# Gated linear attention with a maxout FFN: other score products, paired head parities, and FFN steps given out in thirds

## The chip, the core and the metric

The kernel runs on one core of a Trainium2 chip. The core has five engines that run side by side, each through its own list of instructions in order: TensorE (matmuls; PE in the profile, and PEld for its weight loads), VectorE (DVE), ScalarE (ACT), GpSimd (POOL) and SyncE (SP), whose queue issues all transfers here. They meet only at semaphores: an instruction that waits holds back everything behind it on its own engine. Matmuls write to PSUM, which this kernel cuts into four buffers of two banks; the other engines empty them. The metric is the device time of the program in microseconds (us).

## What is computed

```python
# q, k, v, a_re, a_im: (batch 4, heads 8, seq 768, head_dim 48); w1..w3: (384, 768); w_out: (768, 384)
mag = sqrt(a_re**2 + a_im**2)
scale = minimum(mag, 0.999) / (mag + 1e-6)
ar, ai = a_re * scale, a_im * scale              # a complex gate per step and key channel
for t in range(768):
    S_re, S_im = ar*S_re - ai*S_im + outer(k[t], v[t]), ar*S_im + ai*S_re
    y[t] = q[t] @ S_re
x = y as (4*768 tokens, 8*48)
out = maximum(maximum(x @ w1, x @ w2), x @ w3) @ w_out
```

## The kernel before

The recurrence is worked in chunks of 64 steps. A tile `x` is 128 tokens (two chunks) of one batch element, all 8 heads; a group `g` is two tiles of the same place in two batch elements (x = 2g and y = 2g + 1). There are 24 tiles and 12 groups, and 6 groups follow each other along one sequence.

For each tile there is this work, by the functions of the code:

- `gate_steps`, `turns`, `sines`, `products`: from the gates come log magnitudes `Ln`, running angles (matmuls `cs`), sines `CS`, magnitudes (matmuls `sums`, exponentials `En` and `E`), and with them the keys and queries `Uk` and `Uq`, 112 columns per head. `products(x)[2]` multiplies `Uk` by `En` once the keys have been turned.
- `turn`: PE transposes `Uk` and `Uq` (tiles `tp`), and ACT copies them out to `K` and `Q`.
- `cut`: 16 small matmuls `F` and four exponentials on ACT give `f`, the decay factors between positions within a chunk. Its columns are found by the constants C8 to CD; NF of them in all.
- `prep`, parts 0 to 3 on DVE: `Q`, `K` times factors. They write 16 more columns into `Q` (two products), the keys `KB`, the queries `QB` (two products) and `QG`.
- `scores`: PE makes `A` (from `K` and `Q`, 32 matmuls with 48 columns) and `B` (from `KB` and `QB`, 32 with 80 columns), each into 32 partitions.
- `gather`: DVE moves the blocks that count into the score tile `atm` with masked copies, two from `A` and three from `B`.
- `state`: matmuls `dk` and DVE operations `g` (times the factors, plus `dk`) carry the state on.
- `outputs`: matmuls `y`, 64 per tile, from `atm` with the values `vb` and from `QG` with the state `g`. A pass over 32 output channels that straddles two heads needs two of each kind. ACT copies the result to `xT`.
- The FFN of the group before: `up_step` (three weights by two halves of the 768 channels, 9 matmuls of 128x256 each, then ACT's copy or DVE's maximum into `hT`) and `out_step` (6 matmuls `op`, ACT's copy to `ot`, one transfer out).

A matmul in f32 shows in the profile as two records, so 32 matmuls are x64 there.

The order is written out by hand from group 2 on for PE (`T["chain"]`); on the other engines, and in the groups 0 and 1, a scheduler decides. `group(g)` puts FFN steps between the parts of the attention with `feed(n)`, which takes n steps from a list of eight: one at the start of the group, one after `pairs(x)`, one after the sums, two inside `turning` (ahead of `cs`), two after `pairs(y)`, and one after `turned(y + 1)`. `pairs(x)` is `scores` A, B and `gather` A, B. `turned(x)` is turn keys, turn queries, `cut`, `state` of the tile before, and `prep` part 0. So PE's list in a steady group reads: `op`, A, B, `up`, tp, tp, F, dk, sums, sums, `up`, y, `up`, `up`, cs, A, B, `up`, `up`, tp, tp, F, dk, `op`, y. The exponentials and logarithms of the group after next (`later`, two of three gate steps) stand on ACT between the sines and the copy of the second pair of turned tiles.

A PSUM buffer is handed from use to use. The build fixes which instruction each first matmul waits for: before the change the `up` behind the sums waits for ACT's exponentials `f`, and the `op` behind the second dk waits for ACT's copy `K`.

Of the kernel before, what the change touches and what calls it, by code (L numbers as in the profile page):

```python
# [51 lines left out]
def kernel(  # L52
# [15 lines left out]
    P = 128  # L68
# [15 lines left out]
    C8, C8B, C16, C32, CK, CG, CD, NF = 0, 4, 8, 12, 20, 28, 36, 37  # L84
# [83 lines left out]
    masko = const.tile([P, 4, 32], U8, name="masko")  # L168
# [4 lines left out]
    vbs = [const.tile([P, 2, H // 2, P], FP, name="vb%d" % i) for i in range(4)]  # L173
# [3 lines left out]
    us = {nm: [const.tile([P, H, 2, L64], FP, name="u%s%d" % (nm, i)) for i in range(n)] for nm, n in (("k", 3), ("q", 2))}  # L177
    fs = [const.tile([P, H, 2, NF], FP, name="f%d" % i) for i in range(2)]
    KB = const.tile([P, H, P], FP, name="KB")

    def constants_early():
# [11 lines left out]
        for o in (0, L64):  # L193
            def col(base, n):
                return cuts[o:o + L64, base:base + n]

            between(col(C8, 4), 7, 11, [[16, 4]], [[16, 4]])
            between(col(C8B, 4), 3, 7, [[16, 4]], [[16, 4]])
            vw = col(C16, 4).rearrange("p (n u) -> p n u", u=2)
            between(vw, 15, 19, [[32, 2], [0, 2]], [[32, 2], [8, 2]])  # L200
            vw = col(C32, 8).rearrange("p (i n) -> p i n", i=2)
            between(vw, 15, 35, [[16, 2], [0, 4]], [[0, 2], [8, 4]])
            vw = col(CK, 8).rearrange("p (n u) -> p n u", u=2)
            between(vw, 3, 15, [[16, 4], [8, 2]], [[16, 4], [0, 2]])
            between(col(CG, 8), -1, 3, [[0, 8]], [[8, 8]])

    def constants_late():
# [4 lines left out]
        f = nat1.tile([P, 4, 2, L64], FP, tag="e", padded_shape=[P, 6, 2, L64], name="maskf")  # L212
# [5 lines left out]
        g = f.rearrange("p i c t -> p (i c t)")[:, 0:4 * L64].rearrange("p (i t) -> p i t", i=4)  # L218
        nc.gpsimd.memset(g, 1.0)
        for i, h in enumerate((8, 16, 32, 32)):  # L220
            n, w = L64 // h, h if i < 2 else 16
            o = 16 if i == 3 else 0
            m = g[:, i].rearrange("p (n h) -> p n h", h=h)
            keep(m, -o, [[-2 * h, n], [0, h]], 1)
            keep(m, o + w - 1, [[2 * h, n], [0, h]], -1)
# [21 lines left out]
    def halves(a, g, c, j):  # L247

        b, s = divmod(g, NS)
        t0 = s * P  # L250
        return a[b * C + c, j * 4:(j + 1) * 4, t0:t0 + P, :].rearrange("h (c t) d -> t c h d", c=2)
# [8 lines left out]
    def load_v(g, c):  # L260
        x = g * C + c
        T["v", x] = vbs[x % 4]
        for j in range(2):
            src = halves(v, g, c, j).rearrange("t c (i u) d -> t c i u d", u=2)
            dst = T["v", x][j * L64:(j + 1) * L64, :, 2 * j:2 * j + 2]
            for ch in range(2):
                for u in range(2):
                    nc.sync.dma_start(out=heads(dst[:, ch])[:, :, u], in_=src[:, ch, :, u])
# [122 lines left out]
    def turns(g, cs, meanwhile):  # L391
# [8 lines left out]
        for c in cs:  # L400
            ps = banks("cs", DM)

            for ch in range(2):
                for j in range(2):
                    at = c * DM + j * HC
                    mm(out=ps[j * L64:(j + 1) * L64, ch * HC:(ch + 1) * HC], lhsT=upto[:, ch * L64:(ch + 1) * L64],
                       rhs=w[:, at:at + HC], start=True, stop=True)
# [7 lines left out]
            if (g + 1) % NS > 0:  # L415
                if c == 0:
                    T["carry", g + 1] = nat1.tile([1, W], FP, tag="carry", name="carry")
                for j in range(2):
                    last, at = (j + 1) * L64, c * DM + j * HC
                    nc.sync.dma_start(out=T["carry", g + 1][:, at:at + HC], in_=nf[last - 1:last, HC:])  # L420
# [20 lines left out]
    def both(t, h):  # L441

        return t[:, h].rearrange("p u d -> p (u d)")[:, 0:DD]
# [7 lines left out]
    def products(x):  # L451
        g, c = divmod(x, C)

        def s0():
# [3 lines left out]
            for n, mat in enumerate((mid, rest)):  # L458
                for j in range(2):
                    for ch in range(2):  # L460
                        r = slice(ch * L64, (ch + 1) * L64)
                        at = c * DM + j * HC
                        mm(out=ps[j * L64:(j + 1) * L64, ch, n * HC:(n + 1) * HC], lhsT=mat[r],
                           rhs=T["Ln", g][r, at:at + HC], start=True, stop=True)
# [8 lines left out]
        def s1():  # L473
            for nm in "kq":
                u = T["U" + nm, x] = us[nm][x % len(us[nm])]
                nc.vector.tensor_tensor(out=u[:, :, :, 0:D], in0=T["CS", x], in1=two(hd(T[nm, x])), op=OP.mult)

        def s2():

            u = T["Uk", x][:, :, :, 0:D]  # L480
# [5 lines left out]
    def turn(x, nm):  # L486
# [9 lines left out]
        else:  # L496

            T["Q", x] = un2.tile([P, 4 * H, 48], FP, tag="Q", name="Q")
# [3 lines left out]
    def cut(x):  # L502
# [3 lines left out]
        for i in range(2):  # L506
            for j in range(2):
                for u in range(2):
                    h, o = 4 * j + 2 * i + u, u * L64
# [11 lines left out]
    def prep(x, part):  # L521
# [12 lines left out]
        if part == 0:  # L534
            q8 = rows8(Q[:, :, 32:48])
            times(q8, base.rearrange("p g (n u e) -> p g n u e", u=2, e=8)[:, :, :, 1], C8, 4)
            times(q8, q8, C8B, 4)
        elif part == 1:

            times(*(rows8(t.rearrange("p s (j t) -> p (s j) t", j=2)[:, :, 0:48]) for t in (KB[0:DD], K)), CK, 6)  # L540

            QB = un1.tile([P, 2 * H, 96], FP, tag="QB", name="QB")
            T["KB", x], T["QB", x] = KB, QB
            ends = QB[0:DD].rearrange("p g (s u e) -> p g s u e", s=6, e=8)[:, :, 0::5]
            times(ends, rows8(base[:, :, 16:32]), C16, 4)
        elif part == 2:
            src = Q.rearrange("p (g j) t -> p g j t", j=2)[:, :, 1:2, 0:32].to_broadcast([DD, 2 * H, 2, 32])
            times(T["QB", x][0:DD, :, 16:80].rearrange("p g (i n e) -> p g i n e", i=2, e=8),
                  src.rearrange("p g i (n e) -> p g i n e", e=8), C32, 8)
# [6 lines left out]
    def scores(x, nm):  # L556

        ps = banks(nm)
        for h in range(H):
            for o in range(0, P, 32):  # L560
                c, j = divmod(o // 32, 2)
                if nm == "A":
                    mm(out=ps[o:o + 32, 0, h * 48:(h + 1) * 48], lhsT=T["K", x][0:DD, h, o:o + 32],
                                     rhs=T["Q", x][0:DD, 4 * h + 2 * c + j], start=True, stop=True)
                else:
                    mm(out=ps[o:o + 32, h // HU, h % HU * P:h % HU * P + 80],
                                     lhsT=T["KB", x][0:DD, h, o:o + 32],
                                     rhs=T["QB", x][0:DD, 2 * h + c, 16 * j:16 * j + 80], start=True, stop=True)
        T[nm, x] = ps

    def gather(x, nm):
# [10 lines left out]
        if nm == "A":  # L582
            src = T[nm, x][:, 0, 0:H * 48].rearrange("p (h j t) -> p h j t", h=H, j=1)
            pick(atm.rearrange("p h (j t) -> p h j t", j=2), over(maskd).rearrange("p h (j t) -> p h j t", j=2),
                 src[:, :, :, 0:32].to_broadcast([P, H, 2, 32]))
            pick(atm.rearrange("p h (j n u w) -> p h j n u w", j=2, n=2, u=2)[:, :, :, :, 1],
                 over(masko[:, 0]).rearrange("p h (j n w) -> p h j n w", j=2, n=2),
                 src[:, :, :, 32:48].to_broadcast([P, H, 2, 16]).rearrange("p h j (n w) -> p h j n w", n=2))
        else:
            src = T[nm, x].rearrange("p a (b t) -> p (a b) t", b=HU)  # L590

            pick(atm.rearrange("p h (j u w) -> p h j u w", j=2, u=2)[:, :, :, 1],
                 over(masko[:, 1]).rearrange("p h (j w) -> p h j w", j=2),
                 src.rearrange("p h (s w) -> p h s w", w=16)[:, :, 0:5:4])
            for i in range(2):
                pick(atm[:, :, 32:], over(masko[:, 2 + i]), src[:, :, 16 + 32 * i:48 + 32 * i])

    def state(x):
# [6 lines left out]
        for n in range(H if s < NS - 1 else 4):  # L605
            ch, i = divmod(n, 4)
            for j in range(2):
                r, o = slice(j * L64, (j + 1) * L64), i % 2 * (P - D)
                for lo, hi in ((0, L64), (L64, DD)):
                    mm(out=ps[lo:hi, j, n * D:(n + 1) * D], lhsT=both(T["Uk", x], n)[r, lo:hi],  # L610
                       rhs=T["v", x][r, ch, 2 * j + i // 2, o:o + D], start=True, stop=True)
        dk = ps[0:DD, :, 0:DM].rearrange("p j (c i u d) -> p c j i u d", c=2, u=2, d=D)
# [3 lines left out]
        def four(t):  # L616

            return heads(t).rearrange("p (j i) u d -> p j i u d", j=2)
# [9 lines left out]
    def outputs(x, xs):  # L628
# [4 lines left out]
        for r in range(DM // 32):  # L633
            i, w = divmod(r, 3)
            runs = ((0,), (1, 2), (3,))[w]
            for c in range(2):

                todo = [(n, new) for new in ((True, False) if x // C % NS > 0 or c > 0 else (True,)) for n in runs]
                queues[r % 4] += [(r, c, i, n, new, (n, new) == todo[0], (n, new) == todo[-1]) for n, new in todo]
        for todo in zip(*queues):  # L640
            for r, c, i, n, new, start, stop in todo:
                (j, h), lo = divmod(2 * i + n // 2, 4), 32 * n
                mm(out=y[32 * (r % 4):32 * (r % 4) + 32, r // 4, c * L64:(c + 1) * L64],
                                 lhsT=V[:, c, i, lo:lo + 32] if new else G[0:DD, c, i, lo:lo + 32],
                                 rhs=atm[:, 4 * c + h] if new else QG[0:DD, 2 * (4 * c + h) + j], start=start, stop=stop)
# [8 lines left out]
    def up_step(xs, fs, i):  # L654
        xT, n = T["xT", xs[-1]], len(xs) * P
        if fs[0] == 0 and i == 0:

            T["hT", xs[-1]] = ld2.tile([P, KF, n], FP, tag="ar", name="hT") if xs[0] == 0 else \
                fp2.tile([P, KF, n], FP, tag="hT", padded_shape=[P, KF, TG], name="hT")
        dst = T["hT", xs[-1]][:, fs[0]:fs[-1] + 1]  # L660
        ps = banks("up", len(fs) * n).rearrange("p (f t) -> p f t", t=n)
        for j, f in enumerate(fs):
            for d in range(KD):
                mm(out=ps[:, j], lhsT=ws[i][:, d, f * P:(f + 1) * P], rhs=xT[:, d],
                                 start=(d == 0), stop=(d == KD - 1))
        if i == 0:
            nc.scalar.copy(out=dst, in_=ps)  # L667
        else:
# [208 lines left out]
```

## Time and profile before

| | |
|---|---|
| median of 7 runs | 670.92 us (668.82 to 672.66) |
| the profiled execution, its own time | 669.89 us |
| its span, first to last instruction | 668.2 us |
| PE busy | 591.4 us, 89% of the span |
| DVE busy | 489.3 us, 73% |
| ACT busy | 389.2 us, 58% |
| POOL busy | 121.1 us, 18% |
| span of groups 2 to 9 | about 49 us each |
| DVE busy from 40 to 100 us | 58.2 of 60 us |
| PE busy from 254 to 303 us | 47.8 of 49 us |
| DVE, ACT busy from 254 to 303 us | 38.7, 30.4 of 49 us |

The profile is one execution. Busy time of an engine is read by stretches: the kernel starts with about 110 us in which the weights are rounded and the first tiles are made, then groups of some 49 us follow, and the last 34.6 us are FFN alone on PE. The timeline lists runs of like instructions with their start and length; an entry in brackets is the engine's idle time just before, and who ended it. The chain of waits follows the last instruction back to the first.

### The profile page before, as it was taken

The page shows a single profiled execution, that of the slowest core. Times are in us where ns is not written, and L with a number is a line of the kernel's source. Part 1 is how long each engine was busy: PE and PEld are TensorE (multiplying, and loading weights), DVE is VectorE, ACT ScalarE, POOL GpSimd, SP SyncE. Part 2 cuts the span into 40 slices and gives each one's busy share as a digit, 9 for nine tenths or more (in the row PEclk, how much of TensorE's full clock was granted, in tenths as well). Part 3 has the DMA queues.
Part 4 walks back from the last instruction along what each step waited for, and adds up shares of the span by engine and source line. Part 5 has one row for each costly group of instructions (what it writes and reads, how often), then busy time and mean ns, then how long its engine had stood idle before and what let it go on. Part 6 is the DMA issues. An engine that isn't in the chain of part 4 may idle for free.

```text
span 668.2 us, 25292 instructions
## 1 busy us (share of the span) xinstructions
PE 591.4 (89%) x11228; PEld 480.0 (72%) x11228; DVE 489.3 (73%) x662; ACT 389.2 (58%) x622; POOL 121.1 (18%) x126
## 2 busy tenths in 40 slices
PE   1255768898999999999999999999999999999997
PEld 1144656777867868867868878778778778878785
DVE  4899998978787787787777778787787778755111
ACT  6879687767665665655755854844954944430000
POOL 8400202314023013013023023023023023000000
PEclk9996888999999999999999999999999999999999
DMA  6584544330330420421420421321320210000000
GB/s 139 170 255 93 163 88 82 67 57 16 73 62 15 79 56 15 86 50 26 75 58 20 75 55 21 73 56 21 71 59 14 47 42 2 2 26 3 13 13 24
DMA packets 139052, 39.42 MB, mean 59 GB/s; under 512 B 131648, under 2 KB 134720, under 8 KB 138944
## 3 DMA queue, kind: packets, MB, share of 16 engines
q1 hardware_dynamic: 138944, 37.81, 25.7%
q8 instruction: 88, 1.44, 0.9%
q14 instruction: 20, 0.16, 0.1%
HBM read 33.03 MB, written 4.72 MB: 56 GB/s over the span
## 4 chain that ended last, share of the span: by engine, by line
PE 56%; ACT 18%; issue 5%; DVE 1%; POOL 0%; DMA 0%; POOLq 0%; ACTq 0%
PE up L117 29%; PE op L117 13%; PE y L117 6%; ACT CS L112 2%; ACT K L495 2%; ACT e L112 2%; PE B L117 2%; PE cs L117 2%; ACT L133 2%; PE A L117 1%; DVE Ln L369 1%; ACT ar L383 1%; ACT f L112 1%; ACT e L374 1%; ACT L L112 1%
## 5 line engine op out<-in xcount | busy, mean ns | idle before, releaser
L117 PE MATMUL up<-xT,w 128*128 128x256 f32 (+1 forms) x1404 | 294.3, 367 | 7.4 <-ACT f L112 4.7
L117 PEld LDWEIGHTS up<-xT,w 128*128 128x128 f32 x1404 | 247.2, 190 | 44.4 <-ACT f L112 7.4
L117 PE MATMUL op<-wo,hT 128*128 128x384 f32 x288 | 99.0, 495 | 6.4 <-ACT K L495 6.4
L667 ACT COPY hT<-up 128x768 f32<-128x768 f32 (+2 forms) x27 | 19.6, 726 | 118.9 <-PE up L117 118.9
L117 PEld LDWEIGHTS op<-wo,hT 128*128 128x128 f32 x288 | 53.3, 191 | 41.2 <-ACT K L495 7.4
L669 DVE TENSOR_TENSOR hT<-hT,up 128x768 f32<-128x768 f32 (+2 forms) x54 | 46.4, 859 | 40.1 <-PE up L117 40.0
L527 DVE TENSOR_TENSOR Q<-Q,f 112x512 f32<-112x512 f32 x48 | 39.1, 814 | 48.9 <-ACT f L112 48.9
L379 POOL TENSOR_TENSOR ai<-ai,L 128x768 f32<-128x768 f32 x10 | 22.1, 2211 | 273.2 <-ACT L L112 167.5
L527 DVE TENSOR_TENSOR QB<-Q,f 112x512 f32<-112x512 f32 (+1 forms) x48 | 54.2, 1168 | 0.0
L117 PE MATMUL y<-atm,vb 128*32 128x64 f32 x1536 | 46.1, 228 | 4.7 <-DVE atm L575 4.7
L117 PEld LDWEIGHTS y<-atm,vb 128*32 128x32 f32 x1536 | 39.3, 114 | 14.1 <-issue 11.1
L117 PE MATMUL y<-QG,g 112*32 112x64 f32 x1408 | 45.0, 223 | 0.0
L112 ACT ACTIVATE f<-F 48x296 f32<-48x296 f32 x96 | 39.7, 413 | 0.9
L471 POOL TENSOR_TENSOR k<-E,k 128x384 f32<-128x384 f32 x20 | 25.9, 1296 | 74.1 <-ACT E L112 74.1
L117 PEld LDWEIGHTS y<-QG,g 112*32 112x32 f32 x1408 | 38.4, 113 | 0.0
L527 DVE TENSOR_TENSOR KB<-K,f 112x768 f32<-112x768 f32 x24 | 38.3, 1594 | 0.0
L387 POOL TENSOR_TENSOR ai<-ai,carry 1x768 f32<-1x768 f32 x10 | 21.5, 2154 | 86.8 <-ACT ai L384 80.6
L481 DVE TENSOR_TENSOR uk<-uk,En 128x768 f32<-128x768 f32 x24 | 23.8, 992 | 16.9 <-PE tp L117 16.9
L117 PE MATMUL B<-QB,KB 112*32 112x80 f32 x1536 | 33.3, 242 | 2.7 <-DVE QB L527 2.7
L117 PE MATMUL sums<-Ln,mid 64*64 64x192 f32 x192 | 16.3, 370 | 21.2 <-DVE Ln L369 20.0
L117 PE MATMUL cs<-w,upto 128*64 128x192 f32 x192 | 20.5, 361 | 15.7 <-DVE w L398 15.7
L357 ACT ACTIVATE L<-ai 128x768 f32<-128x768 f32 (+1 forms) x13 | 10.3, 793 | 40.7 <-DVE w L380 32.6
(104 smaller groups left out, 978.7 us busy)
## 6 DMA issues: line engine op xcount, KB each, us to landing
ar<-in_a_re_dram SPq DMA_DIRECT2D x24, 192.0 KB, 3.5
ai<-in_a_im_dram SPq DMA_DIRECT2D x24, 192.0 KB, 3.7
k<-in_k_dram SPq DMA_DIRECT2D x96, 48.0 KB, 2.5
q<-in_q_dram SPq DMA_DIRECT2D x96, 48.0 KB, 2.4
vb<-in_v_dram SPq DMA_DIRECT2D x192, 24.0 KB, 2.1
out_dram<-ot SPq DMA_DIRECT2D x24, 192.0 KB, 1.9
raw<-in_moe_w_dram SPq DMA_DIRECT2D x5, 768.0 KB, 5.9
w<-in_moe_w_dram SPq DMA_DIRECT2D x2, 768.0 KB, 5.6
```

What stands on the lines that cost most here:

```text
L112: tab(nc.scalar.activation(**kw))
L117: ins = f(**kw)
L133: tab(nc.scalar.preload_act_table_set(nm))
L357: nc.scalar.activation(out=L, in_=ai, func=AF.Square)
L379: (nc.gpsimd if g > 1 else nc.vector).tensor_tensor(out=ai, in0=ai, in1=L, op=OP.mult)
L387: nc.gpsimd.tensor_tensor(out=ai[0:1], in0=ai[0:1], in1=T["carry", g], op=OP.subtract)
L471: eng.tensor_tensor(out=hd(T[nm, x]), in0=E, in1=hd(T[nm, x]), op=OP.mult)
L481: nc.vector.tensor_tensor(out=u, in0=u, in1=two(T["En", x]), op=OP.mult)
L495: nc.scalar.copy(out=T["K", x][0:DD].rearrange("p n (j t) -> p j n t", j=2), in_=src)
L527: nc.vector.tensor_tensor(out=out, in0=in_, in1=f.to_broadcast([DD, 2 * H - g, n, 8]), op=OP.mult)
L667: nc.scalar.copy(out=dst, in_=ps)
L669: nc.vector.tensor_tensor(out=dst, in0=dst, in1=ps, op=OP.max)
```

## The change

Four edits are made together.

1. Another split of the scores. `Q` holds 80 columns per 32 tokens in place of 48: the plain queries, and three blocks of 16 columns times factors. They come from three DVE products (512, 1024 and 768 elements per partition) in place of two of 512. `A` takes all 80 columns, and four masked copies on DVE gather from it. `KB` keeps 32 positions per chunk (512 elements in place of 768), `QB` is one product of 512 in place of one of 512 and one of 1024, `B` is 16 matmuls with 32 columns, and two plain copies on ACT move it into `atm`.
2. Heads are paired by parity: partitions 0 to 63 hold even heads, 64 to 127 odd ones. The values of a pair stand side by side in 96 columns, with zeros across, so that a pass over 32 output channels takes one matmul from `atm` also where it straddles two heads: 24 in place of 32 per tile. The queries' loads change their strides; values are loaded by 4 transfers per tile in place of 8 (the same bytes). `cs` and `sums` read their moving rows in four runs of 48.
3. FFN steps are lists of three parts each (one block of 128 channels of an `up`, two of the six matmuls of an `op`), and `feed` counts parts.
4. One part is given out inside `turned`, between the turned queries and `cut`; the step that followed gives its other two parts where it was. Its PSUM buffer stays taken from the first part to the last.

The factors are 35 columns in place of 37, there is one mask less, and `KB` is no longer cleared at the start.

PE's list in a steady group becomes: `op`, A, B, `up`, tp, tp, a third of `up`, F, dk, sums, sums, the rest of that `up`, y, `up`, `up`, cs, A, B, `up`, `up`, tp, tp, a third of `op`, F, dk, the rest of that `op`, y. The waits for PSUM buffers come out as follows: the third of `up` for ACT's copies into `atm`, the second sums for ACT's `f`, the second dk for ACT's copy `K`, the second `tp` for the last masked copy or ACT's copies into `atm`. On DVE, in the groups' second halves, `g` plus `dk` stands behind the first product for `Q`, which waits for `f` (as before); in group 5, the last of its sequence, it stands ahead of it, and in group 6, which starts a sequence, a copy on ACT behind `f` takes its place. On ACT the two copies into `atm` stand behind the first logarithm of the later gate steps, and the copy `K` one place further ahead, in front of the sign.

```diff
-    C8, C8B, C16, C32, CK, CG, CD, NF = 0, 4, 8, 12, 20, 28, 36, 37
+    C8, C16, CB, CK, C32, CG, CD, NF = 0, 4, 12, 18, 22, 26, 34, 35
...
-    vbs = [const.tile([P, 2, H // 2, P], FP, name="vb%d" % i) for i in range(4)]
+    vbs = [const.tile([P, 2, H // 2, 2 * D], FP, name="vb%d" % i) for i in range(4)]
...
-    KB = const.tile([P, H, P], FP, name="KB")
+    KB = const.tile([P, 2 * H, 32], FP, name="KB")
...
     def load_v(g, c):
...
-            src = halves(v, g, c, j).rearrange("t c (i u) d -> t c i u d", u=2)
-            dst = T["v", x][j * L64:(j + 1) * L64, :, 2 * j:2 * j + 2]
             for ch in range(2):
-                for u in range(2):
-                    nc.sync.dma_start(out=heads(dst[:, ch])[:, :, u], in_=src[:, ch, :, u])
+                nc.sync.dma_start(out=T["v", x][j * L64:(j + 1) * L64, ch, :, j * D:(j + 1) * D],
+                                  in_=halves(v, g, c, j)[:, ch])
+
+    def every(view, j):
+        return view.rearrange("p (i u d) -> p i u d", u=2, d=D)[:, :, j]
...
         if part == 0:
-            q8 = rows8(Q[:, :, 32:48])
-            times(q8, base.rearrange("p g (n u e) -> p g n u e", u=2, e=8)[:, :, :, 1], C8, 4)
-            times(q8, q8, C8B, 4)
+            times(rows8(Q[:, :, 48:64]), base.rearrange("p g (n u e) -> p g n u e", u=2, e=8)[:, :, :, 1], C8, 4)
+            two_ = Q[:, :, 32:80].rearrange("p g (s w) -> p g s w", w=16)[:, :, 0::2]
+            src = base[:, :, 16:32].rearrange("p g (v w) -> p g v w", v=1).to_broadcast([DD, 4 * H, 2, 16])
+            times(two_, src, C16, 8)
+            times(rows8(Q[:, :, 48:72]), rows8(Q[:, :, 48:72]), CB, 6)
         elif part == 1:
-            times(*(rows8(t.rearrange("p s (j t) -> p (s j) t", j=2)[:, :, 0:48]) for t in (KB[0:DD], K)), CK, 6)
-            QB = un1.tile([P, 2 * H, 96], FP, tag="QB", name="QB")
...
-            times(ends, rows8(base[:, :, 16:32]), C16, 4)
+            times(rows8(KB[0:DD]), rows8(K.rearrange("p s (j t) -> p (s j) t", j=2)[:, :, 0:32]), CK, 4)
         elif part == 2:
-            src = Q.rearrange("p (g j) t -> p g j t", j=2)[:, :, 1:2, 0:32].to_broadcast([DD, 2 * H, 2, 32])
-            times(T["QB", x][0:DD, :, 16:80].rearrange("p g (i n e) -> p g i n e", i=2, e=8),
-                  src.rearrange("p g i (n e) -> p g i n e", e=8), C32, 8)
+            QB = un1.tile([P, 2 * H, 32], FP, tag="QB", name="QB")
+            times(rows8(QB[0:DD]), rows8(Q.rearrange("p (g j) t -> p g j t", j=2)[:, :, 1, 0:32]), C32, 4)
...
     def scores(x, nm):
+            if nm == "A":
+                for o in range(0, P, 32):
+                    mm(out=ps[o:o + 32, h // HU, h % HU * P:h % HU * P + 80], lhsT=T["K", x][0:DD, h, o:o + 32],
+                       rhs=T["Q", x][0:DD, 4 * h + o // 32], start=True, stop=True)
+            else:
+                for j in range(2):
+                    o = j * L64
+                    mm(out=ps[o:o + 32, 0, h * 32:h * 32 + 32], lhsT=T["KB", x][0:DD, 2 * h + j],
+                       rhs=T["QB", x][0:DD, 2 * h + j], start=True, stop=True)
...
     def gather(x, nm):
...
+            for i in range(2):
+                pick(atm.rearrange("p h (j u w) -> p h j u w", j=2, u=2)[:, :, :, 1],
+                     over(masko[:, 1 + i]).rearrange("p h (j w) -> p h j w", j=2), own(32 + 32 * i, 16))
         else:
-            for i in range(2):
-                pick(atm[:, :, 32:], over(masko[:, 2 + i]), src[:, :, 16 + 32 * i:48 + 32 * i])
+            src = T[nm, x][:, 0, 0:H * 32].rearrange("p (h t) -> p h t", h=H)
+            for o in (0, L64):
+                nc.scalar.copy(out=atm[o:o + 32, :, 32:], in_=src[o:o + 32])
...
     def outputs(x, xs):
-                todo = [(n, new) for new in ((True, False) if x // C % NS > 0 or c > 0 else (True,)) for n in runs]
+                todo = [(V[:, c, i, 32 * w:32 * w + 32], atm[:, 4 * c + i])]
+                for n in ((0,), (1, 2), (3,))[w] if x // C % NS > 0 or c > 0 else ():
+                    todo.append((G[0:DD, c, i, 32 * n:32 * n + 32], QG[0:DD, 2 * (4 * c + i) + n // 2]))
...
     def group(g):
-        ffn = held + ffn_steps(tokens(x - 1))
-        held[:] = [ffn.pop()]
+        ffn = held + every_part(ffn_steps(tokens(x - 1)))
+        held[:] = ffn[-3:]
+        del ffn[-3:]
...
                 turn(x, "q")
+                feed(1)
                 cut(x)
...
-            feed(1)
+            feed(3)
         pairs(x)
...
-        feed(1)
+        feed(3)
         turned(y)
         sums[0]()
         sums[1]()
-        feed(1)
+        feed(2)
         outputs(x, tokens(x))
...
-        feed(2)
+        feed(6)
         turned(y + 1)
-        feed(1)
+        feed(2)
         outputs(y, tokens(y))
```

## The prediction

> **What bounds the kernel now.** I read the page's first two parts, then the chain of waits, then the timelines of TensorE (PE), ACT and DVE in one steady group, then the groups by shape for prices.
>
> ```profile
> span 668.2 us, 25292 instructions
> ...
> PE   1255768898999999999999999999999999999997
> ...
> DVE  4899998978787787787777778787787778755111
> ACT  6879687767665665655755854844954944430000
> ```
>
> Each digit is a tenth of a 40th (16.7 us). Up to about 110 us DVE is full and PE is not; from there to the end PE is at 9. A microsecond of PE work is worth one in most of the span, and nothing in the first 110 us. The chain in group 7 shows where PE waits in spite of that:
>
> ```profile
> 418.42 1.48 PE cs L117 x16
> ...
> 425.11 0.85 ACT L L112
> ...
> 425.99 0.84 ACT w L112
> ...
> 429.30 0.97 DVE Ln L369
> ...
> 431.17 0.94 ACT ar L383
> 432.11 0.91 ACT K L495
> ...
> 433.06 4.14 PE op L117 x12
> 437.20 1.95 PE y L117 x128
> ```
>
> Columns: start, length, what. Between cs and `op` the chain leaves PE: sines, table load, the later gate steps, then the copy `K`, all on ACT but one step on DVE. From the end of cs (419.90) to `op`, ACT sets the time. PE beside it:
>
> ```profile
> 419.80 0.89 PE L117 MATMUL A<-Q,K 112*32 112x48 f32 x64
> 420.51 1.29 PE L117 MATMUL B<-QB,KB 112*32 112x80 f32 x64
> 421.73 8.04 PE L117 MATMUL up<-xT,w 128*128 128x256 f32 x36
> 429.69 0.66 PE L117 MATMUL tp<-ident,uk 64*112 64x64 f32 x16
> ...
> 433.06 4.14 PE L117 MATMUL op<-wo,hT 128*128 128x384 f32 x12 [0.74 <-ACT K L495]
> ```
>
> Starts are closer together than the lengths, since matmuls overlap: A costs 0.71 us from start to start, B 1.22. The idle 0.74 us ahead of `op` is the wait at which the given-out third aims. What follows on ACT and DVE:
>
> ```profile
> 433.81 1.69 ACT L112 ACTIVATE f<-F 48x296 f32<-48x296 f32 x4
> ```
> ```profile
> 435.53 0.69 DVE L527 TENSOR_TENSOR Q<-Q,f 112x512 f32<-112x512 f32 x1 [2.53 <-ACT f L112]
> 436.13 0.55 DVE L626 TENSOR_TENSOR g<-g,dk 112x384 f32<-112x384 f32 x1
> ...
> 437.67 2.58 DVE L527 TENSOR_TENSOR KB<-K,f 112x768 f32<-112x768 f32 x1
> ```
>
> y needs `g`, which stands behind the first product, which waits for `f`. It was there at 436.68, 0.52 us before PE came to y at 437.20.
>
> **The change part by part**, on PE first, per tile.
>
> Scores: A gets 80 columns on 32 partitions, the very shape of B now, so 1.21 us. The new B is 16 matmuls with 32 columns; no row has this shape. Lower bound: half of today's A (0.71/2 = 0.36). Upper bound: today's B unshrunk (1.21), as it has half the matmuls but only two of the four blocks of output partitions, hence less overlap. A's nearest per-matmul price is 0.71/32 = 22 ns with four blocks; with two, and 32 columns for 48, 22 x 2 x 32/48 = 30 ns, times 16 is 0.47. I take 0.5. Sum 1.71 for 1.92: 0.2 us saved (0.35 saved to 0.5 lost).
>
> y: 56 matmuls in place of 64 at 1.95/64 = 30 ns: 0.24 us saved (0 to 0.24). F: 35 columns for 37, nothing worth counting. cs and sums read their rows in runs of 48; the moving rows are as many, I take nothing.
>
> The skill's page "TensorE: Matmul & The Clock Gate", under "Wait — 56ns, not 53.3ns?", speaks against the narrow B: two starts never come closer than about 25 ns, however few columns. A's 64 records start within 0.71 us, 11 ns each, so in these small blocks the trace does not show that floor. By the rule 32 records would cost an estimated 0.8 us, and the sum below would be smaller by 0.3 for about 12 tiles, 3.6 us.
>
> DVE, per tile: products before 512, 512, 768, 512 and 1024 elements, after 512, 1024, 768, 512 and 512: the same 3328 in five instructions. Masked copies go from five to four: 0.43 us less (0.33 in a row). ACT gets two copies of 256 elements from 32 partitions. Nearest row: `hT<-up` of 128x256, 366 ns each; in a row, by E's pair (0.87 for two of 0.49), 0.33 apiece. I take 0.66 for two, bounds 0.5 and 0.94 (the 384-wide copy, 0.47 each). Transfers on SP: four fewer of 24 KB per tile, off the path. Fewer clears and more cut constants on POOL cost about nothing before 20 us, covered by the gates' first steps; uncovered, 8 selects more at 0.2 us are 1.6 us.
>
> Now the wait. **First half of a group** (tp starts at 399.59 in group 7, call it 0). ACT copies `K` and `Q` to 2.61 and makes `f` to 4.30; `up` came at 4.77 there, in the other groups looked at 4.36 to 4.40, and y 4.08 later. After: third of `up` 1.04 to 2.40, F to 2.8, so `f` runs from 3.0 to 4.7. The second sums now needs F's buffer, so it starts at 4.75 and ends at 5.64; the other two thirds take 2.72: y at 8.36 in place of 8.44 to 8.85. I take 0.15 us (0 to 0.5). The wait for `f` has moved from `up` to the sums.
>
> **Second half**, group 7's clock, cs ending at 419.90. ACT: the two copies into `atm` stand behind L (425.11), so w starts about 0.5 late, and with it all up to the last masked input: e<-ar at 430.79. `K` now stands ahead of the sign: 431.54, done 432.53. Sign, `Q`, then `f` from 434.2 to 435.9, 0.4 later than today's 435.50. PE: A, B 1.71 to 421.6, two `up` 7.97 to 429.55, tp 1.04 to 430.6, the third of `op` 1.36 to 431.95, F to 432.4, dk from `K`'s end 432.55 to 433.45, the rest of `op` 2.71 to 436.16. But y waits for `g`: 435.92 plus 0.61 (first product) plus 0.55 gives 437.1. So the 0.74 at `op` returns as 0.94 at y, and y starts 0.1 earlier than before (0.3 later to 0.3 earlier by the copies' bounds). What the narrower B saves in this half is swallowed too. In group 5, where `g` is ahead of the product and dk is half as long (idle today 1.20), y comes 1.4 earlier: 432.55 + 0.45 + 2.71 = 435.7 on this clock. In group 6, where an ACT copy behind `f` makes `g`, 0.2 later.
>
> **Sum.** Groups 2 to 9: pairs of the first tile 0.2, first half 0.15, two y 0.48, together 0.83 x 8 = 6.6; second halves 6 x 0.1 + 1.4 - 0.2 = 1.8. Groups 10 and 11 have no later gate steps, so both pairs count: 1.03 x 2 = 2.1. Group 1: 0.8. The first 110 us: two tiles' masked copies, 0.9 (3 lost to 3 gained, as the scheduler rearranges DVE's list there). The last 34.6 us are unchanged. Total 12.2 us. The profiled execution took 669.89 (span 668.2 and 1.7 around it), so 657.7; the median is 1.0 above that execution: 658.7, rounded to 659. With B at its ends, -0.14 or +0.71 for 12 tiles: 657 to 667.5; with y saving nothing, 24 x 0.24 = 5.8 more.
>
> **The rivals.**
> *Narrow products that are not cheaper.* B stays near 1.21 because half of the output blocks lie idle. For it: sums, dk and F fill four blocks, and no row has two. Against: A's price falls with its columns (0.71 to 1.22 for 48 to 80). +0.71 for 12 tiles is 8.5, and without the early 0.9: 668.5.
> *The gather comes late (slower).* Behind `f`, DVE has one unbroken row: today 435.53 to the last masked copy at 448.40, 12.87 us. After: 435.92 + 12.44 = 448.36, ACT's copies to 449.06, while the next third of `up` wants that buffer at 449.7 (y 437.1, plus 1.7, `op` 4.07, A and B 1.71, `up` 4.08, tp 1.04). Slack: 0.65. POOL's operation stretches whatever DVE runs beside it: KB took 2.58 above, 0.95 alone. If the new products (1024, 768, 512, 512 elements: 3.2 us) all stretch so, that is 5.5 in place of 1.6, so 3.2 past the slack in 8 groups: 659 + 26 = 685. It decides from 2.2 us of extra row (0.65 plus 12.2/8). Against: POOL works about 2.2 us there, as before.
> *The wait is really hidden (faster).* If `f` ends a microsecond earlier than worked out, y starts when PE comes, 436.16: 0.94 in 7 groups, 6.6 us, so 652. For it: ACT idles 1.03 us behind Ln. Against: the two copies stand ahead of that gap, not in it.
>
> **How the numbers follow.** Forecast 64%, not cheaper 13%, late gather 14%, hidden wait 9%. About 0.3% (2 us) is what this kernel's runs can tell from no change. Forecast and hidden wait are faster; of "not cheaper" I count 9 points as no change and 4 as faster: 77, 9 and 14%. The range 652 to 669.5 takes in the hidden wait and the narrow products; the forecast's own is 655 to 664.
>
> **What would show it.** A at 1.2 us and new B at 0.4 to 0.6 from start to start; y in 1.7; no wait of `op` for `K`, but PE idle about 0.9 ahead of the second y, ended by DVE's `g`, except in group 5; the second sums waiting for ACT's `f`; ACT's copies into `atm` at 0.33. I am wrong if B stays near 1.2, or if a first-half third of `up` waits for `atm`.

## The result, and the profile after

The changed kernel takes 674.2 us (median of 18 runs, 672.6 to 676.4) where the kernel before takes 671.1 (43 runs, 668.8 to 674.0): ratio 1.0048, 95% interval 1.0037 to 1.0058. It is slower by 3 us; 12 us less were forecast. One execution of a later run (e9), at 1204 us, is left out of all medians.

First the two rows of the 40 slices that moved most, of the kernel after; each digit is a tenth of 16.9 us, PEclk the granted clock of TensorE.

```profile
PE   1243867898999999999999999999999999999997
...
PEclk9556898898999999999999999999999999999999
```

PEclk before (its PE row stands in the prediction):

```profile
PEclk9996888999999999999999999999999999999999
```

Against the rows before, the third and fourth digit of PE are lower (43 for 55), and of the clock's first ten digits the second, third, eighth and tenth; the rest of PE's row hardly differs. Counted out, PE was busy 109.8 of the first 180 us, before 118.8. To see where the time went, both executions are cut at the starts of `cs`, one in each group:

| | before | after |
|---|---|---|
| profiled span | 668.2 | 674.1 |
| start to group 2's cs | 171.9 | 180.0 |
| from there to the end | 496.3 | 494.1 |
| period of cs, groups 7 to 10 | 49.15 to 49.19 | 49.52 to 49.54 |

The periods repeat within 0.05 us, the start doesn't: spans of one kernel's executions differ by 4 to 5 us. Before's profiled execution was 1.3 us under its median, after's 1.6 over. If the stretch from group 2's cs on is taken as the same in every execution, the median's start is 671.1 - 1.7 - 496.3 = 173.1 us before and 674.2 - 1.7 - 494.1 = 178.4 after. So the start lost 5.3 us, and the rest gained 2.2 in place of some 10. Even the 2.2 are no gain of PE's work: in that stretch before's execution has three idle times of PE that nothing in the profile ends (1.02, 0.60 and 1.22 us, see the last section), together 2.84, and after's has none. Without them the rest is 0.6 longer.

Now a full group. The timeline of PE after, second half of group 7 (start, length, records, idle before):

```profile
425.77 1.31 PE L117 MATMUL A<-Q,K 112*32 112x80 f32 x64
426.90 0.68 PE L117 MATMUL B<-QB,KB 112*32 112x32 f32 x32
...
438.82 1.14 PE L117 MATMUL dk<-vb,uk 64*64 64x48 f32 x64 [0.25 <-ACT K L501]
```

This half came close to the forecast: A takes 1.13 us, the new B 0.62 (`up` follows at 427.52), of the 0.74 us ahead of `op` 0.25 are left ahead of dk, and the next half's tp comes 30.22 us after cs where it came after 30.81. That is 0.59 gained. The loss is in the first half. PE, then ACT, then DVE after (tp starts at 454.54):

```profile
459.41 0.56 PE L117 MATMUL sums<-Ln,mid 64*64 64x192 f32 x8 [0.18 <-ACT f L112]
...
465.88 8.04 PE L117 MATMUL up<-xT,w 128*128 128x256 f32 x36 [1.08 <-DVE g L633]
```
```profile
457.73 1.63 ACT L112 ACTIVATE f<-F 48x280 f32<-48x280 f32 x4
```
```profile
459.39 0.69 DVE L533 TENSOR_TENSOR Q<-Q,f 112x512 f32<-112x512 f32 x1 [3.19 <-ACT f L112]
460.00 0.55 DVE L633 TENSOR_TENSOR g<-g,dk 112x384 f32<-112x384 f32 x1
460.47 1.95 DVE L533 TENSOR_TENSOR Q<-Q,f 112x1024 f32<-112x1024 f32 x1
462.34 1.34 DVE L632 TENSOR_TENSOR g<-g,f 112x384 f32<-112x384 f32 x1
463.61 1.76 DVE L533 TENSOR_TENSOR Q<-Q,f 112x768 f32<-112x768 f32 x1
465.29 0.54 DVE L633 TENSOR_TENSOR g<-g,dk 112x384 f32<-112x384 f32 x1
```

The `up` behind y takes the PSUM buffer that dk held, and the second `g<-g,dk` frees it. That step ends 6.47 us after `f`, and `f` ends 4.82 us after tp: `up` starts 11.34 us after tp. Before, in the same place (tp at 449.16):

```profile
454.56 1.42 DVE L527 TENSOR_TENSOR Q<-Q,f 112x512 f32<-112x512 f32 x1
...
458.85 0.54 DVE L626 TENSOR_TENSOR g<-g,dk 112x384 f32<-112x384 f32 x1
```
```profile
459.54 8.04 PE L117 MATMUL up<-xT,w 128*128 128x256 f32 x36
```

`f` ended 4.30 after tp, the row took 5.93, and `up` came at 10.38 with no wait shown, 0.15 us after the step: the chain already ended where PE's work did, without slack. After, `f` is 0.52 later and the row 0.54 longer, and `up` 0.96 later. The full group: 0.96 lost, 0.59 gained, 0.37 slower. PE waits 1.08 us like this for the second `g<-g,dk` in the first halves of groups 2 to 4 and 7 to 10.

### The profile page after: what moved, and what is told of

It is laid out like the page before. It is cut to its first block, busy times and chain, and to the rows that moved or that the text cites. A ratio compares the mean times of both kernels' runs of the same rounds, so it can differ in the third digit from the quotient of the medians.

```text
span 674.1 us, 22805 instructions
## 1 busy us (share of the span) xinstructions
PE 588.4 (87%) x10076; PEld 469.4 (70%) x10076; DVE 479.4 (71%) x638; ACT 405.8 (60%) x670; POOL 122.5 (18%) x131
## 4 chain that ended last, share of the span: by engine, by line
PE 44%; ACT 27%; DVE 17%; issue 7%; DMA 2%; SPq 2%; POOL 1%; DVEq 0%; POOLq 0%; ACTq 0%
PE up L117 25%; PE op L117 9%; DVE Q L533 6%; ACT f L112 4%; PE y L117 3%; PE A L117 2%; ACT CS L112 2%; ACT Q L505 2%; ACT K L501 2%; PE cs L117 2%; ACT e L112 2%; ACT L133 2%; DVE g L632 2%; DVE g L633 2%; ACT L L112 1%
## 5 line engine op out<-in xcount | busy, mean ns | idle before, releaser
L117 PE MATMUL up<-xT,w 128*128 128x256 f32 (+1 forms) x1404 | 301.0, 371 | 12.9 <-DVE g L633 7.9
L117 PEld LDWEIGHTS up<-xT,w 128*128 128x128 f32 x1404 | 249.3, 192 | 48.7 <-DVE g L633 9.2
L533 DVE TENSOR_TENSOR Q<-Q,f 112x512 f32<-112x512 f32 (+2 forms) x72 | 85.3, 1192 | 59.1 <-ACT f L112 59.1
L117 PE MATMUL A<-Q,K 112*32 112x80 f32 x1536 | 35.2, 249 | 13.4 <-DVE Q L533 13.4
L117 PEld LDWEIGHTS A<-Q,K 112*32 112x32 f32 x1536 | 30.4, 119 | 22.8 <-issue 8.8
L117 PEld LDWEIGHTS y<-atm,vb 128*32 128x32 f32 x1152 | 32.9, 112 | 11.0 <-issue 10.2
L632 DVE TENSOR_TENSOR g<-g,f 112x384 f32<-112x384 f32 x40 | 39.7, 993 | 1.0 <-ACT g L630 1.0
L112 ACT ACTIVATE f<-F 48x280 f32<-48x280 f32 x96 | 38.3, 399 | 3.5 <-PE F L117 2.7
L117 PE MATMUL y<-QG,g 112*32 112x64 f32 x1408 | 39.4, 221 | 0.7 <-ACT g L630 0.3
L477 POOL TENSOR_TENSOR q<-E,q 128x384 f32<-128x384 f32 x20 | 35.2, 1761 | 0.0
L112 ACT ACTIVATE E<-sums 128x384 f32<-128x384 f32 x48 | 22.2, 491 | 18.9 <-POOL q L477 13.3
```

Of the source, the lines that this page charges most:

```text
L112: tab(nc.scalar.activation(**kw))
L117: ins = f(**kw)
L477: eng.tensor_tensor(out=hd(T[nm, x]), in0=E, in1=hd(T[nm, x]), op=OP.mult)
L533: nc.vector.tensor_tensor(out=out, in0=in_, in1=f.to_broadcast([DD, 2 * H - g, n, 8]), op=OP.mult)
L632: nc.vector.tensor_tensor(out=new, in0=four(G[0:DD, c]), in1=F[:, c].to_broadcast([DD, 2, 4, D]), op=OP.mult)
```

## The experiments

Theory 1: the third costs the start. Theory 2: the larger products cost the full groups. Theory 3, formed after the first four runs: a first half ends with the chain F, `f`, first Q product, second `g<-g,dk`, next matmul that wants dk's buffer, and all that lengthens it counts in full. All runs, in us; "to the end" is from group 2's cs, "idle in it" is idle time of PE in that stretch that nothing ends, and the last column is the median's start, worked out as above:

| | median | ratio, 95% | cs of group 2 | to the end | idle in it | period | median's start |
|---|---|---|---|---|---|---|---|
| before | 671.1 | | 171.9 | 496.3 | 2.84 | 49.15 | 173.1 |
| after | 674.2 | 1.004 to 1.006 | 180.0 | 494.1 | 0 | 49.53 | 178.4 |
| e1 no third | 666.6 | 0.991 to 0.996 | 174.8 | 489.5 | 0 | 48.94 | 175.4 |
| e2 third alone | 673.1 | 1.001 to 1.004 | 176.1 | 495.9 | 1.36 | 49.40 | 175.5 |
| e3 scores alone | 669.3 | 0.995 to 0.998 | 174.1 | 493.9 | 2.82 | 49.17 | 173.7 |
| e4 pairing alone | 668.9 | 0.994 to 0.998 | 175.2 | 491.3 | 0.96 | 48.84 | 175.9 |
| e5 state first | 677.9 | 1.006 to 1.013 | 180.8 | 497.5 | 1.90 | 49.77 | 178.7 |
| e6 F first | 684.8 | 1.017 to 1.022 | 179.3 | 503.9 | 0 | 50.32 | 179.2 |
| e7 = e1, state first | 666.4 | 0.990 to 0.995 | 177.1 | 489.2 | 1.71 | 48.53 | 175.5 |
| e8 F and state first | 703.4 | 1.045 to 1.051 | 177.6 | 525.3 | 0 | 54.7 | 176.4 |
| e9 third from group 3 | 672.0 | 0.999 to 1.002 | 175.6 | 494.1 | 0 | 49.52 | 176.2 |
| e10 e5 in first halves | 673.4 | 1.000 to 1.005 | 179.7 | 493.5 | 1.90 | 49.13 | 178.2 |
| e11 e7 in first halves | 665.5 | 0.989 to 0.994 | 176.6 | 490.8 | 1.98 | 48.53 | 173.0 |
| e12 third behind F in first halves | 663.4 | 0.984 to 0.990 | 178.4 | 484.9 | 0 | 48.10 | 176.8 |
| e13 = e12 from group 3 | 663.6 | 0.986 to 0.991 | 177.2 | 484.9 | 0 | 48.10 | 177.0 |
| e14 third to group 2 only | 670.0 | 0.997 to 1.001 | 179.0 | 490.1 | 0 | 48.95 | 178.2 |
| e15 = e13, old scores | 666.9 | 0.992 to 0.996 | 175.3 | 489.2 | 0.99 | 48.48 | 176.1 |

**The three edits apart.** e1 is the change without the third (steps whole again):

```diff
     def turned(x):
-                feed(1)
                 cut(x)
```

> The changed kernel without the step that is given out between the turned queries and the sums for the factors; the new blocks of scores and the new pairing of heads stay. Theory 1 (the third of an FFN step loses the start): up to group 2's cs about 7 us come back, a steady group stays as in the changed kernel, so 666 to 668 us against 671 before. Rival (the start's 8 us come from the larger products and from ACT's copies into atm, whatever stands in between): 673 to 676. In both the wait of `up` for the second g<-g,dk after the first half's y stays.

666.6: the third alone is worth 7.6 us, and without it the change gains 0.6%. Theory 1 stands in size, but not in place: the full groups gain too, 48.94 for 49.53, which theory 1 left as they were. e2, e3 and e4 take the parts of the diff one at a time (thirds and their place; scores, masks, factors; pairing, loads, y).

> The kernel before with FFN steps in thirds alone: old scores, old pairing. Theory 1 in its narrow form (the third waits for a buffer that ACT's new copies free late): here DVE's last masked copy frees it, early enough, so the start loses nothing and the time is 669 to 672. Theory 1 in its wide form (the third costs the start by its place alone): 676 to 680. In steady groups the wait of `op` for K goes and comes back as a wait of y for g.

Between its two ranges. Group by group: +0.24 us in a full group, and 2.4 us of start although no ACT copy stands in the way, so neither form of theory 1 holds alone.

> The kernel before with the new blocks of scores alone (and the layout of the turned keys and queries without a gap, which makes the room for it): old pairing of heads, whole FFN steps. Theory 2 (the larger second and third product put the second g<-g,dk late, and `up` after the first half's y waits for its buffer): about 1 us lost in each of groups 2 to 9 and nothing gained on y: 677 to 682. Rival (the products cost nothing on the path): 669 to 672.

Theory 2's price fails, 2 us are gained: the full group stays at 49.17, where A and B together are 0.2 us shorter, twice, and the longer row on DVE takes as much back.

> The kernel before with the new pairing of heads alone: y in 56 matmuls of whole rows of v, one transfer of v less in each quarter; old scores, whole FFN steps. If y is worth what it showed in the changed kernel (1.39 for 1.94 us) and nothing takes its place: 0.55 us twice in each of 10 groups, so 659 to 662. If y's end only moves into the next wait (for g<-g,dk's buffer in the first half, which had no slack before): half of it, 664 to 667. If nothing comes of it: 670 to 672.

668.9 lies between its second and third range. The expectation took y's gain from a stretch where part of y had run before it waited for `g`. From its first record to the next `up` y takes 1.73 us (e12) for 1.95, 0.22 less; for the 19 tiles of the stretch to the end that is 4.2; without the idle times 3.1 were gained there (493.5 to 490.4). The start was 2.8 later.

**The chain.** What makes up the 0.59 that the third costs per group is in e1's ACT row (tp at 447.52):

```profile
450.12 1.63 ACT L112 ACTIVATE f<-F 48x280 f32<-48x280 f32 x4
```

`f` starts 2.60 after tp, with the third 3.19: 0.59, and `up` comes 0.57 earlier. Two things held it, either of which would have done so alone. F ends 3.09 after tp where it ends 1.60 after in e1, and in e2 `f` waits for it, 0.43 us. And ACT reached `K` 0.58 later, since its copies into `atm` waited for DVE's masked copies. This second part isn't the third's place alone: in e1's second halves the scheduler also put one `g<-g,dk` ahead of the first Q product (at 432.36), out of the row that the masked copies close. The next runs shorten the chain at either end. e5 puts the state's steps first on DVE:

```diff
+            if c in (C16, CK, C32) and "chain" in T and T.get("last") is not None:
+                tc.add_manual_dep(ins.ins, T["last"].ins.name, order, reason="state first")
```

> The changed kernel, with both steps of the state on DVE (g<-g,dk twice) put ahead of the second and third Q product and of KB and QB, from group 2 on. Theory 3 (the end of a first half is set by the chain F, f, first Q product, second g<-g,dk, next matmul that wants dk's buffer): the idle 1.08 us ahead of `up` goes, the period of groups 3, 4 and 8 to 10 falls from 49.53 to 48.4 to 48.6 us, the start stays as it is, the time is 664 to 667 us. Rival (the products that now come 1.1 us later make A or the masked copies late instead): 671 to 675.

The rival was right on the cause, and the time is 3 us above its range: the 1.08 is gone, but A of the second pair waits for its last Q product, and y, which now gets dk's buffer, for the same `g`:

```profile
450.68 1.31 PE L117 MATMUL A<-Q,K 112*32 112x80 f32 x64 [0.60 <-DVE Q L533]
...
465.69 0.32 PE L117 MATMUL y<-atm,vb 128*32 128x64 f32 x8 [0.67 <-DVE g L636]
```

e6 is the change with the third moved:

```diff
-                feed(1)
                 cut(x)
+                feed(1)
```

> The changed kernel, with the third of the FFN step behind the sums for the factors (F) in place of ahead of them; everything else as changed. Theory 3: f ends about 0.6 to 0.9 us earlier in each half, and so does the second g<-g,dk: the wait of `up` for it falls from 1.08 to 0.2 to 0.5 us, the period to 48.7 to 49.0; in groups 1 and 2 F no longer stands behind the third either, which gives back 2 to 4 us of the start: 664 to 668 us. Theory 1 (it is the buffer that the third waits for, wherever the third stands): the start stays at 180.0 and the time is 670 to 673.

A miss by 17 us. `f` did end early (4.25 after tp), but the DVE row behind it took 6.69, and `up` still waited 1.00 us. In the second half the third of `op` now waits 0.69 for a buffer that DVE's maximum into hT frees, which delays dk, and y waits 0.75 for `g`. F first is not enough, and in the second half it is wrong.

> The changed kernel without the third and with the state's two steps ahead of the products on DVE. Theory 3: the idle 0.60 us ahead of `up` goes, the 0.44 us in which `up` waits for f stays: period 48.94 to about 48.4, 661 to 664 us. Rival as for the run with the third: 666 to 669.

The period came down to 48.53 as expected, but the stretches that end with cs of groups 5 to 7 gained nothing, and one near the end took 50.28, 1.71 of it idle: the stretch to the end is only 0.3 shorter, and the median stays, in the rival's range.

> All that the theories point to: the third behind F and from group 2 on alone (the first groups give out whole steps, as before), the state's two steps ahead of the products. Theory 3: no wait for f or for g<-g,dk is left in a first half, the period is 47.9 to 48.3 us, the start that of the run without the third (group 2's cs at 174 to 176 us): 656 to 660 us. If the waits only move again: 663 to 667.

The largest miss (703.4 for 656 to 660), and no test of the theory: with the steps pinned in second halves too, the scheduler put two gate steps in among them, and A waits for a Q product behind them. DVE there, in one group:

```profile
511.19 0.96 DVE L382 TENSOR_TENSOR w<-w,L 128x768 f32<-128x768 f32 x1
512.07 2.16 DVE L635 TENSOR_TENSOR g<-g,f 112x384 f32<-112x384 f32 x1
514.15 0.95 DVE L383 SCALAR_TENSOR_TENSOR w<-w,ai 128x768 f32<-128x768 f32 x1
```

The last Q product starts only at 518.83, and A waits 3.27 us for it. Behind that wait A, B and `up` ran at a granted clock of 0.65 and took 8.62 us up to the next tp, 5.82 in e12: the wait cost nearly twice its length. So e10 to e12 pin the first halves alone (`x % C == 1`), and e12 gives the third there alone, behind F, from group 2 on.

> The changed kernel, with the state's two steps ahead of the second and third Q product on DVE in the first halves alone, where the run with both halves lost at A in the second. Theory 3: A no longer waits for Q; the 1.08 us ahead of `up` go, at most 0.3 come back as y's wait for dk's buffer: period 48.7 to 49.1, start as changed (180 us): 668 to 671. Rival (the third's price is not in this chain): period 49.5, 673 to 676.

> The changed kernel without the third, the state's two steps ahead of the products in the first halves alone. Theory 3: period 48.53 in every full group, as the run with both halves had it in most, without that run's loss of 1.7 us in one group at the end: 662 to 664 us. Rival (pinning is worth nothing): 666 to 667.

> The third in first halves alone, behind F, from group 2 on; second halves give out whole steps; the state's two steps ahead of the products in the first halves. Theory 3: with F ahead of the third, f ends as early as without it, the third fills what was `up`'s wait of 0.45 us for f: period 48.1 to 48.3, group 2's cs at 174 to 177: 658.5 to 662. If the third makes dk and with it the state late instead: 663 to 667.

The periods are 49.13, 48.53 and 48.10, each as theory 3 gave it (e10 0.03 over, as 0.67 of its 1.08 came back as y's wait for `g` where 0.3 were allowed). The times are 1.4 to 2.4 us over, so those of e10 and e12 lie in their rivals' ranges: it is the periods and the waits that speak for theory 3, not the times. Around groups 5 and 6 one or two stretches gained nothing in e10 and e11, one group near the end was long in both (last section), and e12 lost 1.4 us of start against e1. e12's first half, tp at 447.80, DVE and the `up` behind y:

```profile
455.11 0.56 DVE L636 TENSOR_TENSOR g<-g,dk 112x384 f32<-112x384 f32 x1
455.58 1.43 DVE L533 TENSOR_TENSOR Q<-Q,f 112x1024 f32<-112x1024 f32 x1
```
```profile
457.73 1.35 PE L117 MATMUL up<-xT,w 128*128 128x256 f32 x5
```

The state is done 7.87 us after tp, and `up` comes at 9.93, unheld: 1.41 earlier than with the change. e12 is 1.3% faster than the kernel before and 1.6% (663.4 to 674.2) than the changed one.

**The start.** PE, then ACT in group 1 after:

```profile
112.26 0.94 PE L117 MATMUL up<-xT,w 128*128 128x128 f32 x6 [1.63 <-ACT atm L603]
113.63 0.57 PE L117 MATMUL F<-cuts,Ln 64*48 64x35 f32 x32 [0.44 <-ACT ot L699]
```
```profile
110.74 0.84 ACT L359 ACTIVATE L<-ai 128x768 f32<-128x768 f32 x1 [2.71 <-POOL ai L381]
111.49 0.72 ACT L603 COPY atm<-B 32x256 f32<-32x256 f32 x2
```

In groups 1 and 2 the third wants a buffer that ACT's copies into `atm` free; these stand behind a gate step that waits for POOL, and F stands behind the third. e9 gives whole steps up to group 2:

> The changed kernel, with whole FFN steps in the start and in groups 1 and 2; the third is given out from group 3 on alone. If the third costs the start because it waits there for a buffer: group 2's cs at 174 to 176 us as without the third (180.0 changed), then the changed kernel's period of 49.5 from group 3 on: 668.5 to 671. If the start's loss is of the new scores and the scheduler's list: 673 to 676.

```profile
110.99 0.56 PE L117 MATMUL F<-cuts,Ln 64*48 64x35 f32 x32
```

F comes 2.85 us after its tp (108.14), with the third 4.11 after (109.52). The stretches that end with cs of groups 1 and 2 took 46.8 and 49.3 us for 48.7 and 50.8, so 3.4 less in the profile, 0.8 of it a shorter idle time that nothing ends (last section); in the median 2.2 are gained (672.0, between the two ranges). e14 is the complement:

> The changed kernel with the third in the start and in groups 1 and 2 alone, whole steps from group 3 on (the complement of the run with the third from group 3 on). If start and steady groups add up: group 2's cs at about 180, then the period without the third, 48.94: 669 to 671 us. If the start's loss is scatter between executions or of the list: 666 to 668.

Inside its range: 670.0, 3.4 us over e1, with the period of e1. Early third 3.4 and late third 5.5 (e9 less e1) make 8.9 where both together cost 7.6: nearly additive, within the start's scatter.

> As the run with the third behind F in first halves, but third and order of the state's steps from group 3 on alone, groups 1 and 2 as without the third. If the 51.02 us of group 2 there came from the third (without it: 49.2): 1 to 2 us less, 661 to 662.5 us, period 48.10 from group 3 on. If group 2 was slow by its gate steps anyway: 663 to 664.

The stretch to group 2's cs fell from 51.0 to 49.2 as expected, but the one that ends with group 0's cs was 1.1 longer, and the median is e12's: nothing gained. Nor is the 1.8 a price of waits: PE was busy 47.3 us of that stretch in e12 and 45.4 in e13 with the same 858 records, at granted clocks of 0.90 and 0.93.

> The kernel of the run from group 3 on, with the scores as they were before (A of 48 columns, B of 80, masked copies alone): new pairing, third behind F in first halves, the state's steps ahead of the products. If the new scores gain nothing once the chain is mended (A and B together 1.74 for 1.94 us, but in a half where `op` waits for dk or K anyway): period 48.2 to 48.5, 661 to 664. If they are worth their 0.2 us twice a group and more: 48.5 to 48.9, 664 to 667.

48.48 and 666.9: the new scores are worth 0.38 us per group and 3.3 us in all, once the chain is mended; the period lies on the edge of both ranges, the time in the second.

## Why the prediction was wrong

Right, by its own steps: A and B (1.13 and 0.62 for 1.21 and 0.5, so 0.2 saved per pair); y (1.73 for 1.70); ACT's copies (0.36 each for 0.33); in the first half `f` at 4.82 (4.7) and the second sums at 4.87 (4.75); in the second half K, `f`, `g`, and `op` behind y 20.33 us after cs (437.1 plus 1.7 is 20.45). That last number is right by luck, on another path: PE was to idle 0.9 us ahead of this y, but y starts unheld 18.35 us after cs (18.75), as its first rows ran before `g` was done, and takes 1.98 us. The narrow B goes at 0.62/32 = 19 ns from record to record, so the estimate by the Trainium skill's "TensorE: Matmul & The Clock Gate", section "Wait — 56ns, not 53.3ns?" (no two starts closer than about 25 ns), was too high here, as A had suggested.

The step that failed is the one that closes the first half: "y at 8.36 in place of 8.44 to 8.85. I take 0.15 us", with y's own 0.24 added. y came 8.47 us after tp, where the kernel before, at the same place, has 8.43: the 0.15 was gone already. And the working followed the half to the start of y and stopped there. Behind y, `up` wants dk's buffer, and what frees it hangs on `f` with a whole DVE row between. The timeline of before shows the step ending 0.15 us ahead of that `up`. Neither gain reached the end, and the 0.5 us by which `f` was rightly seen to come later, together with 0.54 of longer row, came through: 0.96 lost for 0.39 gained. With the second half's 0.05 of gain above its forecast that is 1.3 us short per full group. Counted without the idle times, six stretches from cs to cs (to groups 3, 4 and 7 to 10) are each short by this, 7.8 us of the 10.5 between the 9.9 forecast from group 2's cs on and the 0.6 lost; 1.1 lie between the cs of groups 5 and 6 and 1.5 behind group 10's. In the stretch to group 5's cs, where `up` doesn't wait for `g`, 0.8 of the 0.9 forecast came.

The row was mis-sized too: "the same 3328 in five instructions" holds for the sum, but the larger product moved ahead of the second state step, 1.95 us where one of 1.42 stood. It stands where POOL works: the 1024-wide Q product took 1.95 us beside POOL here, 1.22 in the second half. The Trainium skill's "GPSIMD Engine Reference", section "1. Specifications", says that GpSimd shares its SBUF interfaces with VectorE and contends with DVE instructions of two SBUF inputs; these rows agree, and no run here takes POOL's work away. POOL is not what lengthened the row, though: the product of 512 before was stretched by the same 0.73 us there (1.42, alone 0.69).

The start was priced at 0.9 and group 1 at 0.8 of gain; 5.3 were lost. The sign "a first-half third of `up` waits for `atm`" was named as what would prove me wrong, and it came in groups 1 and 2, for another reason than the late-gather rival gave: not stretched products but ACT's place behind POOL. 2 to 3.5 us of the start are this (e9, e14). Another 2 are lost without the third (e1), also with the pairing alone (e4), not with the scores alone (e3). In e1 they stand for the most part in one stretch, to group 2's cs: 49.2 us for 46.9. There the second tp waits 1.78 us for DVE's masked copies (0.46 before), the 8 us from 153.56 on ran at granted clocks of 0.60 and 0.54, and PE was busy 45.5 us with 858 records at a mean clock of 0.93, before 43.4 us with 954 at 1.00. So a longer wait and the slower clock behind it fit e1's loss in size. In e4 it lies elsewhere, in the stretch to group 1's cs (49.4 for 47.1). No run tests the clock, and why the copies come later is open.

## What to carry to other kernels

Follow a moved step past the next consumer to the first matmul that takes a buffer freed at the end of the chain it delays; a step put ahead of the head of a chain delays all of it, even if it fills a wait. Where a chain has no slack, reorder the engine in its middle in the same edit, only in the half that needs it, and look what the scheduler puts in the gap. Put the granted clock beside every stretch that is compared: a wait can cost more than its length. Give each half of a loop its own place for filler work: the same third gained behind F in first halves and lost there in second halves.

## What was not expected of the hardware

Four runs with pinned state steps (e5, e7, e10, e11) show one long group near the end, e11's of 52.2 us for 48.5. PE stood idle for 1.71 to 1.98 us with nothing that ended it, and in e11 the granted clock fell after it. Two windows of e11 behind the idle time (window, length, then busy us and records of PE, PEld, DVE, ACT and POOL, granted clock, DMA share, GB/s):

```profile
510.00:512.00 2.00, 2.00 (x7) 1.57 (x6) 2.00 (x4) 0.00 (x0) 0.00 (x0) 0.50 0.17 33
512.00:514.00 2.00, 2.00 (x8) 1.63 (x7) 1.18 (x2) 0.00 (x0) 0.00 (x0) 0.65 0.00 0
```

The idle 1.98 us cost 3.7 in the group, as four microseconds of `up` behind it ran at 0.50 and 0.65. In e10 a like hole of 1.90 us was followed by a clock of 1.00. The kernel before has holes of 1.02 us in group 3, 0.60 in group 7 and 1.22 in group 11. Kernels that share code have them at the same place and of like length, each in its one trace: ahead of A in group 11 1.22, 1.36, 1.28, 0.96 and 0.99 us (before, e2, e3, e4, e15), within y near 95 us 1.57 to 1.60 (after, e5, e6, e10, e14) or 0.73 to 0.75 (e7 to e9, e11 to e13). That speaks for the program and against chance. In the windows around the holes of e10 and e11, packets of the DMA queue for instructions are seen; that a hole is a wait for them was not tried.
